# Second feed-forward chunk on two levels of Strassen's scheme, part of the weight conversion on ScalarE and GpSimd, one output block by two adding DMAs

## The chip, the cores and the metric

The kernel runs on one core of a Trainium2 chip. The metric is the device time in microseconds (us) of one execution. Three runs of the kernel before gave 2347.29, 2343.07 and 2347.35 us, a median of 2347.29. The engines named here: TensorE (PE, with its weight loads PEld), VectorE (DVE), ScalarE (ACT), GpSimd (POOL), and SyncE (SP), which only issues DMAs. An engine works off its own instructions in the order in which they were laid down.

## The reference

All data are float32 except two weight matrices, which arrive as float64. For 8 batches of 448 tokens, attention with 12 heads of 64 is computed with a mix over heads before and after the softmax; its result is a tensor x of 8 x 448 x 768. Then:

```
X     = fft(fft(x, axis=1), axis=2)
u     = x + real(X)
un    = (u - mean(u)) / sqrt(var(u) + 1e-6)          # over the last axis
ch    = maximum(un @ w_ch1, 0) @ w_ch2               # w_ch1 768 x 3072, w_ch2 3072 x 768
out   = u + ch
```

The change lies in the last two lines, the feed-forward part.

## The kernel before, in words

`mix_phase` computes the attention, the Fourier mix and u, and writes u to DRAM. It fills the first 812 us of the span, up to the first matmul of line 1169. `ffn_phase` does the rest.

**Tiling.** The 3072 hidden features are cut into NC = 6 chunks (index c), the 3584 tokens into NTB = 7 blocks of 512 (index t). The loop runs over n = 7c + t: chunk by chunk, and inside a chunk block by block. One such n is called a step.

**A step** has two halves. `first` (lines from 1144 on) multiplies a block of normalized tokens, `ub`, with a chunk of w_ch1, `w1`. It uses one level of Strassen's scheme (in Winograd's form): seven products in the order `ORDER`, each of 12 matmul records of 256 columns (line 1169) and accumulated in three kinds of PSUM banks, P, Q and R. Between the products ScalarE copies banks out or applies Relu, and VectorE adds (L1187, L1190, L1195). From the four blocks of h it then forms sums (L1215, L1216, L1219, L1230). The second half multiplies h with a chunk of w_ch2, `w2`:

- `second`, for chunks 0 and 1, does seven products of 384 columns (L1249). In chunk 0 VectorE adds each to the tokens' u (L1256), and SyncE stores the result to the output. In chunk 1 ScalarE and VectorE collect blocks in tiles `od` (L1265 to L1269), and GpSimd sends each by a DMA that adds to what lies in the output (L1271).
- `second2`, for chunks 2 to 5 (`c >= DEEP`, `DEEP = 2`), splits each of the seven products again by Strassen's scheme: 7 x 7 = 49 products of 192 columns (L1306). For this it needs quarters' sums of h (tiles `hq`, function `quarters`, L1133, by VectorE and GpSimd) and, once per chunk, sums of w2 (tiles `wt`, function `halves`, L1142: four subtractions for each of the seven, alternately on VectorE and GpSimd, in the chunk's first step). ScalarE empties most banks into `od` tiles (`take`, L1334; `begin`, L1325), VectorE adds the others (`more`, L1328) and sums whole `od` tiles (`both`, L1337), and GpSimd sends four adding DMAs (`out_`, L1340). `second2` lays its work down in numbered slots, one matmul a slot; slots from 49 on are interleaved with the next step's `first` (`SEAM`, `beside`). `od` has nine buffers.

**The weights' conversion.** The class `_Weights` turns float64 weights into float32 and forms the seven Strassen operands; the result goes to DRAM and is loaded a chunk later by `load_w1` and `load_w2`. A *part* is one 128-row slice of a chunk: three parts for w1 and two for w2 per chunk. A part has four *pieces* of 128 x 256 (w1) or 128 x 384 (w2). Each piece is loaded raw (`load`, L225, `ahead` pieces in advance) and takes seven VectorE operations on its high and low words: absolute value of the high word (`begin`, L247), range limits (`clamp`, L251), shift (L255), sign (L261), power (L265), low word (L269), sum (L273). Four sums per part (L279) follow, and stores to DRAM (L233). These VectorE operations stand in a list; `deal(k)` lays down the next k of them. In chunks 2 to 5, `DEALS` says how many follow each product of `first`, for a chunk's first step and for the others. The parts of chunk 1 are worked in chunk 0, and later parts as lists run short. The raw loads and stores are GpSimd's DMAs up to chunk 1 and SyncE's after that (`wts.eng`).

**What sets the order.** In the two-level steps the order on TensorE, VectorE, ScalarE and GpSimd is the one written in the program; SyncE's DMAs, and before that ScalarE and GpSimd too, are placed by a planner that goes by its own estimates of when something is ready. The first step of the feed-forward part fixes TensorE, VectorE, GpSimd and SyncE; then, up to the end of chunk 1, only TensorE and VectorE are fixed.

Of the kernel before, what the change touches and what calls it, by code (L numbers as in the profile page):

```python
# [165 lines left out]
class _Weights:  # L166
# [14 lines left out]
    def open(self, ctx, tc, ahead=1):  # L181
        self.ahead = ahead
# [4 lines left out]
        self.praw, self.ptmp, self.pst = pool("wraw", ahead + 1), pool("wtmp", 1), pool("wst", 1)  # L187
# [24 lines left out]
    def add(self, c, n):  # L212
# [25 lines left out]

        def begin(k):
# [6 lines left out]
            box["top"] = new(slot)  # L246
            vec.tensor_scalar(box["tmp"].bitcast(U32), box["hi"], 0x7fffffff, None,  # L247
                              op0=ALU.bitwise_and)

        def clamp():  # L250
            vec.tensor_scalar(box["tmp"], box["tmp"], _f32(0x38000000),  # L251
                              _f32(0x47efffff), op0=ALU.max, op1=ALU.min)

        def shift():
            vec.tensor_scalar(box["top"].bitcast(U32), box["tmp"].bitcast(U32),  # L255
                              0x07ffffff, 3, op0=ALU.bitwise_and,
                              op1=ALU.logical_shift_left)
# [23 lines left out]

        self.ops.append((lambda: load(k0 + self.ahead - 1), False))
# [718 lines left out]
DEEP = 2  # L1001
DEALS = ((0, 2, 2, 2, 2, 0, 0), (2, 3, 3, 3, 3, 0, 0))
# [5 lines left out]
def ffn_phase(ctx, tc, rest, ident, u_scr, u_rev, wts, ub_scr, out, fold_rest,  # L1008
# [14 lines left out]
    wts.open(ctx, tc, 3)  # L1023
    once = ExitStack()

# [118 lines left out]
    def first(n, st, beside):  # L1144
# [12 lines left out]
        for k, i in enumerate(ORDER):  # L1157
# [54 lines left out]
            elif i != 2:  # L1212
                wts.deal(2 if norms else 3 if c == 0 else 4)
# [19 lines left out]
    def second(n, st):  # L1233
        c, t = divmod(n, NTB)
        h = st["h"]
        u = us[t] if c == 0 else None
        os = {}
        norms = c == 0 and t + 1 < NTB
# [4 lines left out]
        for k, i in enumerate(ORDER):  # L1243
            for x in range(NT2 // 2):
# [3 lines left out]
                for kf in range(FM):  # L1248
                    nc.tensor.matmul(p, h[:, LHS[i], kf, x * P:(x + 1) * P],  # L1249
                                     w2[i][:, kf, :], start=i in (0, 4, 1)[:3 - (c > 0)] and kf == 0,  # L1250
                                     stop=kf == FM - 1, skip_group_check=True)
                r, d = DEST[i]
                last = i in (1, 6, 2, 3)
                if c == 0:
                    us_ = u[2 * r + x][:, d * DH:(d + 1) * DH]
                    nc.vector.tensor_tensor(us_, us_, p, op=ALU.add)  # L1256
                    if last:
                        nc.sync.dma_start(out=acc[t, r, d][:, x, :], in_=us_)
                    continue
                if (r, d) not in os:  # L1260
                    os[r, d] = right["od"].tile([P, 2, DH], F32, name="od", tag="od")
                o = os[r, d][:, x, :]
                if i == 0:
                    q = ps["Q", x] = ps_tile("Q")
                    nc.scalar.copy(out=q[:, :DH], in_=p)  # L1265
                elif i in (4, 5, 1, 3):
                    nc.scalar.copy(out=o, in_=p)
                else:
                    nc.vector.tensor_tensor(o, o, p, op=ALU.add)  # L1269
                if last and x == 1:  # L1270
                    nc.gpsimd.dma_start(out=acc[t, r, d], in_=os[r, d][:, :, :],  # L1271
                                        accum_op=ALU.add)
# [6 lines left out]
            if n == 0 and k > 2:  # L1279
                next_part()  # L1280
            wts.deal(2 if norms and k >= NT2 else 4)
            if t == NTB - 1:
                load_w2(c + 1, i)

    def second2(n, st):
# [119 lines left out]
    for n in range(DEEP * NTB):  # L1405
        c, t = divmod(n, NTB)
# [13 lines left out]
        if c == 0:  # L1420
            wts.deal(1000)
# [102 lines left out]
```

## Time and profile before

The profile is of one execution of 2343.49 us, of which its span is 2341.7 us.

| what | us |
|---|---|
| median of the runs | 2347.29 |
| profiled execution | 2343.49 |
| its span | 2341.7 |
| PE busy in the span | 2281.3 |
| DVE, ACT, POOL busy | 1677.4, 1101.0, 1140.6 |
| chunk 1, first product's end to the same of chunk 2 | 1111.98 to 1365.94 |
| chunk 2, likewise | 1365.94 to 1609.89 |
| chunk 3, likewise | 1609.89 to 1852.26 |

Busy time by stage, in us, by windows of the trace:

| window | PE | DVE | ACT | POOL | DMA share |
|---|---|---|---|---|---|
| 1109.2 to 1363.2 (chunk 1) | 253.64 | 181.34 | 62.25 | 98.93 | 0.84 |
| 1366 to 1610 (chunk 2) | 241.63 | 173.62 | 104.87 | 88.90 | 0.64 |
| 1610 to 1852 (chunk 3) | 239.34 | 177.13 | 104.65 | 93.02 | 0.64 |
| 1852 to 2094 (chunk 4) | 239.95 | 181.45 | 105.04 | 96.08 | 0.64 |
| 2094 to 2341 (chunk 5) | 237.62 | 142.36 | 103.57 | 98.11 | 0.51 |

How to read the rows that follow: a group's row names line, engine, operation, written tile and read tiles, shapes, the count, busy time and mean. A row of the timeline gives start and length in us, then the same, and in brackets how long the engine was idle before it and what ended that. A float32 matmul appears as two records. A TensorE row that ends a little after the next one starts is normal, since matmuls are pipelined. The profile's line numbers are those of the kernel before.

### The profile page before, as it was taken

How to read it: one execution, taken by the hardware profiler on the slowest of the kernel's cores; microseconds unless marked ns; L12 is line 12 of the kernel's file. 1: busy time of each engine (PE TensorE's matmuls, PEld its weight loads, DVE VectorE, ACT ScalarE, POOL GpSimd, SP SyncE). 2: the span in 40 equal slices, each digit the busy share in tenths (PEclk: the TensorE clock that was granted, in tenths of full speed). 3: DMA queues.
4: the chain of work that ended last, by engine and by line, in shares of the span. 5: the costliest groups of instructions: out<-in, count | busy, mean ns of one | idle time of the engine just before them, and what ended most of it. 6: DMA issues, size and time to landing. Idle time of an engine off the chain costs nothing.

```text
span 2341.7 us, 59482 instructions
## 1 busy us (share of the span) xinstructions
PE 2281.3 (97%) x22600; PEld 1717.1 (73%) x22600; DVE 1677.4 (72%) x3596; ACT 1101.0 (47%) x3085; POOL 1140.6 (49%) x1692
## 2 busy tenths in 40 slices
PE   6999999999999989999999999999999999999998
PEld 3455555555555667676777779998999899999998
DVE  3778887887887747775676766778776777776556
ACT  4776767676676522221222234344344344444434
POOL 3587967878778622210343443335333533443333
PEclk9999999999999999999999999999999999999999
DMA  7565664756656475658787966648645955684553
GB/s 159 157 181 175 182 175 152 205 168 182 186 156 198 146 242 181 220 185 298 209 229 211 270 202 180 161 135 259 172 123 159 267 128 156 176 236 103 147 129 67
DMA packets 213481, 425.60 MB, mean 182 GB/s; under 512 B 39080, under 2 KB 135744, under 8 KB 213198
## 3 DMA queue, kind: packets, MB, share of 16 engines
q1 hardware_dynamic: 141758, 278.78, 35.0%
q0 software_dynamic: 65440, 141.05, 27.5%
q8 instruction: 181, 2.97, 0.5%
q10 hardware_dynamic: 6000, 1.97, 0.5%
q14 instruction: 102, 0.84, 0.1%
HBM read 213.16 MB, written 129.39 MB: 146 GB/s over the span
## 4 chain that ended last, share of the span: by engine, by line
PE 87%; DMA 4%; DVE 4%; ACT 2%; issue 1%; POOL 1%; SPq 1%; ACTq 0%; DVEq 0%; POOLq 0%
PE psP L1169 18%; PE psP L1306 10%; PE psR L1169 9%; PE mx L616 6%; PE psP L1249 6%; PE ms L680 6%; PE ms L588 5%; PE psR L1306 5%; PE psQ L1169 5%; PE po L650 5%; PE psR L1249 3%; DMA Kr<-Sb 3%; PE psQ L1306 3%; PE ms L805 2%; PE psQ L1249 1%; PE ms L562 1%
## 5 line engine op out<-in xcount | busy, mean ns | idle before, releaser
L640 POOL TENSOR_SCALAR PP<-PP,rcp 128x448 f32<-128x448 f32 x368 | 235.2, 648 | 196.8 <-DVE rcp L638 165.6
L630 ACT ACTIVATE PP<-mx,nmx 128x448 f32<-128x448 f32 x368 | 230.2, 631 | 186.5 <-DVE nmx L623 176.2
L623 DVE TENSOR_REDUCE nmx<-mx 128x1 f32<-128x448 f32 x368 | 213.4, 618 | 128.6 <-PE mx L616 126.3
L1340 POOL DMA_DIRECT2D out_dram<-od x109 | 133.1, 1406 | 283.5 <-DVE od L1337 160.2
L1133 POOL TENSOR_TENSOR hq<-h 128x256 f32<-128x256 f32 (+1 forms) x168 | 104.6, 623 | 291.0 <-ACT h L1191 171.5
L1337 DVE TENSOR_TENSOR od<-od 128x768 f32<-128x768 f32 x196 | 189.0, 975 | 52.4 <-ACT od L1334 50.5
L616 PE MATMUL mx<-Kr,kw 60*32 60x448 f32 x2944 | 212.5, 549 | 11.6 <-DMA Kr<-Sb 11.1
L588 PE MATMUL ms<-kT,qT 64*32 64x448 f32 (+1 forms) x3072 | 202.7, 547 | 8.6 <-ACT qT L451 6.0
L663 DVE STREAM_TRANSPOSE Pv<-po 128x896 f32<-128x896 f32 x184 | 203.8, 1108 | 4.3 <-PE po L650 2.1
L451 ACT COPY Sb<-ms 124x448 f32<-124x448 f32 (+1 forms) x384 | 184.3, 540 | 36.4 <-PE ms L588 23.7
L650 PE MATMUL po<-PP,kw 60*32 60x448 f32 x2944 | 195.7, 538 | 0.0
L1334 ACT COPY od<-psP 128x192 f32<-128x192 f32 x390 | 124.8, 320 | 147.2 <-PE psP L1306 142.9
L680 PEld LDWEIGHTS ms<-Pv,vv 64*64 64x64 f32 x5376 | 137.1, 132 | 68.9 <-issue 52.3
L225 POOL DMA_DIRECT2D raw<-in_moe_w_ch_dram x88 | 52.1, 592 | 264.6 <-DVE tmp L269 247.2
L1169 PE MATMUL psP<-qs,w1t 128*128 128x256 f32 x744 | 177.3, 379 | 0.0
L1169 PE MATMUL psP<-ks,w1t 128*128 128x256 f32 x744 | 176.8, 379 | 0.1
L680 PE MATMUL ms<-Pv,vv 64*64 64x120 f32 (+1 forms) x5376 | 158.9, 263 | 0.0
L1249 PE MATMUL psP<-w2t,h 128*128 128x384 f32 x448 | 155.5, 491 | 0.4 <-DVE od L1269 0.4
L1169 PEld LDWEIGHTS psP<-ks,w1t 128*128 128x128 f32 x744 | 139.9, 190 | 18.5 <-DVE u L1256 0.7
L1169 PEld LDWEIGHTS psP<-qs,w1t 128*128 128x128 f32 x744 | 139.8, 190 | 17.5 <-issue 0.2
L1190 DVE TENSOR_TENSOR h<-h,psP 128x512 f32<-128x512 f32 x42 | 28.8, 687 | 142.0 <-PE psP L1169 141.8
L1169 PE MATMUL psP<-ub,w1t 128*128 128x256 f32 x528 | 126.4, 379 | 0.0
(194 smaller groups left out, 5127.4 us busy)
## 6 DMA issues: line engine op xcount, KB each, us to landing
Kr<-Sb SPq DMA_DIRECT2D x736, 105.0 KB
out_dram<-od POOLq DMA_DIRECT2D x137, 384.0 KB, 6.3
qs<-ub SPq DMA_DIRECT2D x89, 384.0 KB
ks<-ub SPq DMA_DIRECT2D x88, 384.0 KB
ub<-ub SPq DMA_DIRECT2D x79, 384.0 KB
w1t<-w SPq DMA_DIRECT2D x42, 384.0 KB
w2t<-w SPq DMA_DIRECT2D x42, 384.0 KB
raw<-in_moe_w_ch_dram POOLq DMA_DIRECT2D x56, 256.0 KB, 4.4
```

The source lines that it names most:

```text
L588: nc.tensor.matmul(pss[x][o:o + hi - lo, :S], st["qT", xx][64 * x:64 * x + 64, y, lo:hi], st["kT", xx][64 * x:64 * x + 64, y, :], start=Tr ...
L616: nc.tensor.matmul(mx[x][64 * z + o:64 * z + o + 32, :S], kw1[64 * x:64 * x + KR, o:o + 32], Kr[64 * x:64 * x + KR, z, :], start=True, sto ...
L623: nc.vector.tensor_reduce(nmx[:, :], steps[T]["mx"][x][:, :S], axis=AX.X, op=ALU.max, negate=True)
L630: nc.scalar.activation(steps[T]["PP"][:, x, :], steps[T]["mx"][x][:, :S], ACTF.Exp, bias=steps[T]["nmx", x][:, :], accum_out=steps[T]["den ...
L640: nc.gpsimd.tensor_scalar(PP[:, x, :], PP[:, x, :], rcp[:, x:x + 1], 1.0, op0=ALU.mult, op1=ALU.mult)
L650: nc.tensor.matmul(po[o:o + 32, z, :S], kw2[64 * z:64 * z + KR, y, :], PP[64 * z:64 * z + KR, :, c * HS:(c + 1) * HS], start=True, stop=True)
L663: nc.vector.transpose(turned[a]["Pv"][:, j, :].rearrange("p (z s) -> p z s", z=2), steps[T]["po"][:, :, :S])
L680: nc.tensor.matmul(pss[y][64 * x:64 * x + 64, :nu * R], st["v", pr][64 * y:64 * y + 64, x, jb * D:(jb + 1) * D], _ap(Pv, 64 * y * rp + 32 ...
L1169: mm = nc.tensor.matmul(p[:, m, :], w1[i][:, kc, m * P:(m + 1) * P], ub[:, kc, :], start=i in (0, 4, 1)[:3 - seed] and m == kc == 0, stop= ...
L1249: nc.tensor.matmul(p, h[:, LHS[i], kf, x * P:(x + 1) * P], w2[i][:, kf, :], start=i in (0, 4, 1)[:3 - (c > 0)] and kf == 0, stop=kf == FM ...
L1306: nc.tensor.matmul(ps[j, key][:, :DQ], a, b, start=m in (0, 4), stop=True, skip_group_check=True)
L1337: eng.tensor_tensor(D[j][:, :, :], D[j][:, :, :], D[k][:, :, :], op=ALU.add)
```

## The change

Four things are changed together.

1. `DEEP` goes from 2 to 1, so chunk 1 too uses `second2`; `second` then serves chunk 0 alone, and its branch for chunk 1 is deleted. The tiles for two levels were opened ahead of chunk 1 before, and still are.
2. `_Weights` gets a mode `split`, used from chunk 1 on. A piece's absolute value is made by ScalarE (`Abs`, straight into the piece's tile), its range limits are set by GpSimd in place, and the other five operations stay on VectorE. The two new operations of a piece are laid down when the piece two before it begins on VectorE. The weight pools are closed and opened again behind chunk 0, with five raw buffers for four, raw loads four pieces ahead instead of three, and two buffers for each finished tile instead of one.
3. The deals change: `DEALS` rises to 10 operations in a chunk's first step and 18 in the others (8 and 14 before), chunk 0 takes one part in each step from 1 to 6 (1 to 5 before), and parts are added when the list is shorter than 36 instead of 14.
4. Output block 21 (`(1, 0)` in the code) is the sum of `j3` and `j6`. Before, VectorE added the two and one DMA added the sum to the output. Now `j3` and `j6` are each sent by an adding DMA, at slots 27 and 44, and block 22 is summed in `j4` instead of `j6`. The last step of all is as before.

```diff
+    def open(self, ctx, tc, ahead=1, split=False):
+        self.ahead, self.split = ahead, split
...
+        self.pst = pool("wst", 1 + split)
...
+        def early(k):
+            _, f, slot = ps[k]
+            top = new(slot)
+            tops.append(top)
+            nc.scalar.activation(top, self.raws[k0 + k][:, :f, 1].bitcast(F32), ACTF.Abs)
+            clamp(nc.gpsimd, top)
+
         def begin(k):
             _, f, slot = ps[k]
             load(k0 + k + self.ahead)
...
+            if self.split:
+                while self.pre and self.pre[0][0] <= k0 + k + 2:
+                    self.pre.pop(0)[1]()
+                box["top"] = tops[k]
+            else:
+                box["top"] = new(slot)
+                size(vec, box["hi"], box["tmp"])
...
-            self.ops.append((lambda k=k: begin(k), True))
-            for fn in (clamp, shift, sign, power, lower, whole):
+            self.ops.append((lambda k=k: begin(k), not self.split))
+            if not self.split:
+                self.ops.append((lambda: clamp(vec, box["tmp"]), True))
+            self.ops.append((lambda: shift(vec, box["top" if self.split else "tmp"],
+                                           box["top"]), True))
+            for fn in (sign, power, lower, whole):
...
-DEEP = 2
-DEALS = ((0, 2, 2, 2, 2, 0, 0), (2, 3, 3, 3, 3, 0, 0))
+DEEP = 1
+DEALS = ((2, 2, 2, 2, 2, 0, 0), (3, 4, 4, 4, 3, 0, 0))
...
-    wts.open(ctx, tc, 3)
     once = ExitStack()
+    wts.open(once, tc, 3)
...
             for s, *o in ((33, j5, j0), (40, j6, j5), (47, j5, j4), (54, j0, j1),
-                          (61, j5, j2), (62, j3, j6), (63, j6, j4)):
+                          (61, j5, j2), (62, j4, j6)):
                 on(s, both, vec, *o)
+            on(27, out_, j3, 1, 0)
+            on(44, out_, j6, 1, 0)
             on(55, out_, j0, 0, 0)
             on(62, out_, j5, 0, 1)
-            on(63, out_, j3, 1, 0)
-            on(64, out_, j6, 1, 1)
+            on(63, out_, j4, 1, 1)
...
-    for n in range(DEEP * NTB):
-        c, t = divmod(n, NTB)
-        if c == 0 and 0 < t < NK + FM + 1:
-            wts.add(*parts_.pop(0))
-        while c and sum(o[1] for o in wts.ops) < 52:
+    for n in range(NTB):
+        if n:
             wts.add(*parts_.pop(0))
...
         if n == NTB - 1:
             once.close()
+            wts.open(ctx, tc, 4, True)
...
-            while parts_ and sum(o[1] for o in wts.ops) < 14:
+            while parts_ and sum(o[1] for o in wts.ops) < 36:
```

More of the change, by code (lines that the diff above doesn't have):

```diff
@@ L179, in __init__ @@
         self.ops, self.pieces, self.raws, self.later = [], [], {}, []
-    def open(self, ctx, tc, ahead=1):
-        self.ahead = ahead
+        self.pre = []
+    def open(self, ctx, tc, ahead=1, split=False):
+        self.ahead, self.split = ahead, split
         def pool(name, bufs):
@@ L186, in pool @@
                                                   reuse_waits="tile"))
-        self.praw, self.ptmp, self.pst = pool("wraw", ahead + 1), pool("wtmp", 1), pool("wst", 1)
+        self.praw, self.ptmp = pool("wraw", ahead + 1), pool("wtmp", 1)
+        self.pst = pool("wst", 1 + split)
     def _parts(self, c):
@@ L233, in store, with size, clamp, shift @@
             self.later.append(lambda: self.eng.dma_start(out=dst[slot], in_=box[slot]))
+        def size(eng, hi, tmp):
+            eng.tensor_scalar(tmp.bitcast(U32), hi, 0x7fffffff, None,
+                              op0=ALU.bitwise_and)
+        def clamp(eng, tmp):
+            eng.tensor_scalar(tmp, tmp, _f32(0x38000000), _f32(0x47efffff),
+                              op0=ALU.max, op1=ALU.min)
+        def shift(eng, tmp, top):
+            eng.tensor_scalar(top.bitcast(U32), tmp.bitcast(U32), 0x07ffffff, 3,
+                              op0=ALU.bitwise_and, op1=ALU.logical_shift_left)
+        def early(k):
[4 more added lines that the diff above has]
+            clamp(nc.gpsimd, top)
         def begin(k):
@@ L245, in begin @@
             box["slot"] = slot
[L246 to L257, printed above, removed]
+            if self.split:
[5 more added lines that the diff above has]
+                size(vec, box["hi"], box["tmp"])
         def sign():
@@ L280, in total @@
             store(o)
+        tops = []
+        if self.split:
+            self.pre.extend((k0 + k, lambda k=k: early(k)) for k in range(len(ps)))
         self.ops.append((lambda: load(k0 + self.ahead - 1), False))
         for k in range(len(ps)):
-            self.ops.append((lambda k=k: begin(k), True))
-            for fn in (clamp, shift, sign, power, lower, whole):
+            self.ops.append((lambda k=k: begin(k), not self.split))
[4 more added lines that the diff above has]
+            for fn in (sign, power, lower, whole):
                 self.ops.append((fn, True))
@@ L1212, in first @@
             elif i != 2:
-                wts.deal(2 if norms else 3 if c == 0 else 4)
+                wts.deal(2 if norms else 3)
             if i == 2:
@@ L1231, in first, with second @@
         assert not beside
-    def second(n, st):
-        c, t = divmod(n, NTB)
[L1235 to L1238, printed above, removed]
+    def second(t, st):
+        h, u = st["h"], us[t]
+        norms = t + 1 < NTB
         if norms:
@@ L1249, in second @@
                     nc.tensor.matmul(p, h[:, LHS[i], kf, x * P:(x + 1) * P],
-                                     w2[i][:, kf, :], start=i in (0, 4, 1)[:3 - (c > 0)] and kf == 0,
+                                     w2[i][:, kf, :], start=i in (0, 4, 1) and kf == 0,
                                      stop=kf == FM - 1, skip_group_check=True)
                 r, d = DEST[i]
[L1253 to L1272, printed above, removed]
+                us_ = u[2 * r + x][:, d * DH:(d + 1) * DH]
+                nc.vector.tensor_tensor(us_, us_, p, op=ALU.add)
+                if i in (1, 6, 2, 3):
+                    nc.sync.dma_start(out=acc[t, r, d][:, x, :], in_=us_)
             if norms and k < NT2:
@@ L1278, in second @@
                 total(t + 1, k - NT2 + 1)
-            if n == 0 and k > 2:
+            if t == 0 and k > 2:
                 next_part()
@@ L1282, in second @@
             if t == NTB - 1:
-                load_w2(c + 1, i)
+                load_w2(1, i)
     def second2(n, st):
@@ L1404, in ffn_phase @@
     parts_ = [(c, k) for c in range(1, NC) for k in range(NK + FM)]
-    for n in range(DEEP * NTB):
-        c, t = divmod(n, NTB)
-        if c == 0 and 0 < t < NK + FM + 1:
-            wts.add(*parts_.pop(0))
-        while c and sum(o[1] for o in wts.ops) < 52:
+    for n in range(NTB):
+        if n:
             wts.add(*parts_.pop(0))
@@ L1419, in ffn_phase @@
         second(n, st)
-        if c == 0:
-            wts.deal(1000)
+        wts.deal(1000)
         if n == 0:
```

## The prediction

> **What bounds the kernel now.** I began with the page's shares and its list of costliest groups. TensorE is busy for 97% of the span, so a change pays only if it shortens TensorE's work or removes or adds a stall of TensorE.
>
> ```profile
> PE 2281.3 (97%) x22600; PEld 1717.1 (73%) x22600; DVE 1677.4 (72%) x3596; ACT 1101.0 (47%) x3085; POOL 1140.6 (49%) x1692
> ```
>
> Next came the chain that ended last, for the pace of one token step. A row here is start, length, and twelve matmul records, that is one product of the first matrix; the same tile recurs once a step.
>
> ```profile
> 1254.15 2.59 PE psP L1169 x12
> ...
> 1290.34 2.59 PE psP L1169 x12
> ...
> 1438.67 2.59 PE psR L1169 x12
> ...
> 1472.88 2.59 PE psR L1169 x12
> ```
>
> In feed-forward chunk 1 a step takes 1290.34 - 1254.15 = 36.19 us; in chunk 2, which already runs two levels, 1472.88 - 1438.67 = 34.21 us (34.20 over most pairs). This agrees with the timeline: one product of the first matrix is 2.59 us, so seven are 18.13; seven one-level second products of 2.58 us are 18.06; the 49 small ones start 0.325 us apart, 15.93 in all. The two-level form is thus shorter on this array by about 2.0 us a step, though it issues 49 matmuls of 192 columns for 28 of 384.
>
> Last came TensorE's own waits in the two-level chunks, by its timeline. The bracket holds the idle time and what ended it.
>
> ```profile
> 1387.90 0.59 PE L1306 MATMUL psP<-wt,h 128*128 128x192 f32 x2 [2.37 <-DVE od L1328]
> 1632.14 0.59 PE L1306 MATMUL psP<-wt,h 128*128 128x192 f32 x2 [2.66 <-DVE od L1328]
> 1873.89 0.59 PE L1306 MATMUL psP<-wt,h 128*128 128x192 f32 x2 [2.05 <-DVE od L1328]
> 2115.41 0.59 PE L1306 MATMUL psP<-wt,h 128*128 128x192 f32 x2 [1.82 <-DVE od L1328]
> ```
>
> There is one such stall per two-level chunk, always in its first step, where VectorE works off four extra subtractions (L1142) behind the sums of h before it can empty a PSUM bank. Chunk 5 has no weight pieces left to convert and still stalls 1.82 us; the others lose 2.05 to 2.66. No other step of these chunks waits, but for the last at the very end.
>
> **Part 1, chunk 1 on two levels.** Seven steps at 36.19 - 34.20 = 1.99 us: 13.9 us gained. Against it stands the first step. From psR to psR the steps that hold a stall last 38.53 (n = 14), 37.14, 36.52 and 36.29 us, that is 4.3, 2.9, 2.3 and 2.1 over 34.20. At n = 14 the excess is more than its 2.37 us of idle: the matmuls behind the gap are 0.64 us apart instead of 0.325, for 3 us.
>
> ```profile
> 1389.83 0.85 PE L1306 MATMUL psR<-w2t,hq 128*128 128x192 f32 x2
> 1390.47 0.85 PE L1306 MATMUL psP<-w2t,h 128*128 128x192 f32 x2
> ```
>
> The granted clock of 1380 to 1400 us is 0.91 as a mean, while the stall of 2.66 us cost only itself. The Trainium skill ("TensorE: Matmul & The Clock Gate", section "Why this matters for your kernels") asks only that idle gaps stay under about 3 us; by it the new first step would cost 2.4 and the part would bring 11.5 before the seams. The row shows that 2.4 us of idle can bring half rate, so I go by the row. I price the first step of chunk 1 like n = 14 (4.3), which loads a fresh set of weights behind a one-level chunk just the same; n = 14 becomes an ordinary one (2.9), and the 0.63 us that chunk 1 lost at its own end goes (1111.98 to 1365.94 is 253.96; seven steps are 253.33). Sum: 13.9 - 4.3 + (4.3 - 2.9) + 0.6 = **11.6 us gained**. The same from chunk lengths: 253.96 + 243.95 before, 243.95 + 242.37 after.
>
> **Part 2, weight pieces off VectorE.** Of 25 parts, 6 are now done in chunk 0; 19 parts of 4 pieces, 76 pieces, are left. Each sheds two VectorE operations, 0.29 + 0.29 us uncontended at 256 columns (0.36 + 0.36 at 384), and gains one ScalarE and one GpSimd operation. Abs has no row. The nearest is the 128x384 copy, 478 ns (L1267); [...]0.5 to 1 us, and I take 0.5. A table load before each Abs would be the bad bound: the one load in the trace took 1.28 us, and two per piece would be 195 us. I count none: one load serves Exp, Copy, Relu and Identity here, and the skill ("ScalarE: Activation LUTs", "Table sets: the hidden batching unit") lists abs in every set. The clamp on GpSimd I take from L640, 648 ns for 448 columns: 0.4 to 0.6 us. Some 2.2 pieces a step mean 1.1 us more on ScalarE (43% busy, 104.65 of 242 us in chunk 3) and 1.2 on GpSimd (38%).
>
> What does this do on TensorE's path? VectorE must be ready for h22 when product 6 ends. Its spare time there is shown by its timeline, with eleven weight operations dealt before it and with none:
>
> ```profile
> 1725.93 0.69 DVE L1190 TENSOR_TENSOR h<-h,psP 128x512 f32<-128x512 f32 x1 [4.36 <-PE psP L1169]
> ...
> 2140.79 0.69 DVE L1190 TENSOR_TENSOR h<-h,psP 128x512 f32<-128x512 f32 x1 [7.72 <-PE psP L1169]
> ```
>
> The new deal is fifteen there, from the dearer kinds: 15 x 0.37 = 5.5 us (256 columns) or 15 x 0.48 = 7.2 (384). With one 0.96 us sum less (part 3), 7.72 + 0.96 - 5.5 = 3.2 or 1.5 us is spare. VectorE is slowed while GpSimd works (L1142 on VectorE takes 0.74 us beside GpSimd, 0.35 alone), but 1.2 us of clamps cannot eat more than the rest. So ordinary steps: zero. In first steps ten operations replace eight, one sum goes: +4.0 - 2.9 - 0.96 = +0.1 us per chunk, between -0.5 and +1; I take zero. If the cover went, every late microsecond would delay h21's sums and so the bank that product 0 waits for, as in the rows above.
>
> The waits that come with it: an Abs stands on ScalarE behind its raw load, and the PSUM copies stand behind the Abs. Its load is issued four pieces ahead and the Abs runs two ahead, so in one step the load has ten VectorE operations' room, some 5 to 8 us; raw loads landed in 4.4 us (median). The Abs that can be short of data fall in products 5 and 1, when ScalarE's next item is a Relu with over 2 us to spare. Zero, with the bad end in the rivals.
>
> **Part 3, block 21.** One 128x768 sum on VectorE goes (0.96 us a step, off the path), an accumulating DMA of 384 KB is added to each two-level step but the last. Its issue costs GpSimd 1.22 us, at slots 27 and 44, where GpSimd is idle:
>
> ```profile
> 1714.28 1.21 POOL L1340 DMA_DIRECT2D out_dram<-od  x1 [9.38 <-DVE od L1337]
> ```
>
> Both DMAs add to the same bytes. The skill ("DMA: Bandwidth & Descriptors", "Two DMAs through the same engine are not ordered") says that a queue does not order them and the issuer has to wait for the first to land; that speaks against the edit. The row: landing takes 6.3 us, the issues are 17 x 0.325 = 5.5 us apart, so GpSimd, with the sum block for j0 behind it at slot 55, would stand about 2 us of some 9 idle. By rule and by row the sum gets zero; uncovered it would be 2 us a step. The DMA engines are 64% busy in chunks 2 to 4 and 84% in chunk 1, whose four adding DMAs become five: no stage is DMA-bound.
>
> **Part 4, the seam from chunk 0.** Chunk 0 takes one more part in its last step, about 32 x 0.45 = 14 us of VectorE where it now has an 8 us gap and GpSimd 37.75 us; zero. Afterwards the pools are reopened, so the chain of raw load, Abs, clamp, shift starts empty in step 7. The SP queue issues the last w2 load of chunk 0 at 1109.42, TensorE begins step 7 at 1109.39; if the raw loads follow and land like the w2 load of the other seam,
>
> ```profile
> 1347.27 9.19 DMA w2t<-w
> ```
>
> the first piece is there at about 1118.6. ScalarE's Abs would hold h21's copy, due 1119.6, by about a microsecond; VectorE would start its ten dealt operations (3.7 us), two sets of L1142 (3 to 4) and two sums (1.4) then, ending near 1127.5 against 1124.9, when h21's product ends: 2.6 us late. If the planner puts the raw loads ahead of the waiting w2 loads, as it did at 1363.85, it is nothing. Also, the planner may pull the first L1142 set into chunk 0's tail (in the trace VectorE stood 5.36 us for w2 at the other seam, which cost TensorE 0.36). Bounds 0 and 8; I take **1.5 us lost**.
>
> **Sum.** 11.6 - 1.5 = 10.1 us. In the profiled execution 2343.5 (span 2341.7 and 1.8 around it) becomes 2333.4; against the median of 2347.3, which lies 3.8 above that execution, **2337.2**.
>
> **Rivals.** (a) The seam is dear: step 7 stalls 8 us for raw and w2 data and a further half-rate stretch follows, while the first steps of all chunks grow by 1 us: 11.6 - 8 - 2 gives 2346, at best 2342. For it: 2.7 MB of w2 and 1 MB of raw in one place; against: chunk 1's own start shows no wait. (b) ScalarE becomes the gate, and the kernel is slower. Place: products 0 to 4 of each step, Abs waiting for raw data on SP behind ub loads that keep TensorE's pace (one per 2.59 us). If the Abs delays PSUM copies so that TensorE loses 0.33 us in each of 35 steps, the gain is gone; at 0.8 us it is 28 - 11.6, near 2364. For it: load and Abs are only two pieces apart; against: ScalarE's idle of about 2 us between copies in every product. (c) More is gained: the first-step stall falls to chunk 5's 1.82 everywhere and no half rate follows; 11.6 + 3.4 gives 2332. (d) Part 1 saves nothing since the array is not the limit: the step times of 36.19 and 34.20 speak against it; folded into (a).
>
> **How the numbers follow.** Forecast 0.63 (its own range 2333 to 2342), (c) 0.06, (a) with (d) 0.18, of which 0.12 still faster, 0.05 the same, 0.01 slower; (b) 0.13, of which 0.02 the same, 0.11 slower. About 0.2%, 4.7 us, is what a measurement can tell from no change. Faster 0.81, same 0.07, slower 0.12. The range must take in the forecast and nearly all of (a): 2332.5 to 2346; it leaves out (b) and some of (c).
>
> **What would show it.** Chunk 1's steps at 34.20; one stall before a `psP<-wt,h` matmul in step 7 and in each later first step, 1.8 to 2.7 us; VectorE idle before L1190's counterpart at 1.5 to 3.2 us; no table load but the first; GpSimd waiting for a landing at slot 44 with nobody behind. Wrong if TensorE waits for ScalarE copies in ordinary steps, or if step 7 loses over 8 us.

## The result, and the profile after

The kernel after takes 2334.98 us (median of 17 runs, 2326.71 to 2340.21); the kernel before, run on the same chips beside it, takes 2344.55 us (17 runs). The ratio is 0.9954 with a 95% interval of 0.9942 to 0.9967: faster by 0.46%. Applied to the 2347.29 us of the runs shown before, that is 2336.5 us; predicted were 2337.2. The profiled execution of after lasts 2333.72 us, with a span of 2332.0, that is 9.7 less than before. Line numbers below are those of the kernel after, in which L1310 is the matmul of the second level (L1306 before), L1192 the product of the first matrix (L1169), L1332 `more` (L1328) and L1213 the sum of h22 (L1190).

The shares of the page:

```profile
PE 2272.2 (97%) x22894; PEld 1752.2 (75%) x22894; DVE 1704.3 (73%) x3629; ACT 1176.3 (50%) x3336; POOL 1279.8 (55%) x1783
```

TensorE has 294 matmul records more (two for each of 147 matmuls) and is busy 9.1 us less. GpSimd, busy for 139 us more, is the engine that took the work. The chain that ended last shows the pace of chunk 1 (start, length, twelve records of one product):

```profile
1289.77 2.59 PE psR L1192 x12
...
1323.97 2.59 PE psR L1192 x12
```

These are the same product in two successive steps: 34.20 us, where the kernel before took 36.19 there. TensorE's stalls, from its timeline (the bracket is the idle time before the row and what ended it), are again one per first step of a chunk, now five (what it waits for in the very last step is left out):

```profile
1136.39 0.78 PE L1310 MATMUL psP<-wt,h 128*128 128x192 f32 x2 [2.27 <-DVE od L1332]
1379.62 0.59 PE L1310 MATMUL psP<-wt,h 128*128 128x192 f32 x2 [1.81 <-DVE od L1332]
1621.22 0.92 PE L1310 MATMUL psP<-wt,h 128*128 128x192 f32 x2 [1.91 <-DVE od L1332]
1864.41 0.59 PE L1310 MATMUL psP<-wt,h 128*128 128x192 f32 x2 [1.81 <-DVE od L1332]
2105.91 0.59 PE L1310 MATMUL psP<-wt,h 128*128 128x192 f32 x2 [1.80 <-DVE od L1332]
```

They are about as short as chunk 5's was before (1.82), except the one at n = 7. Two of the five are followed by matmuls at half rate. Busy time by windows around the first three of these rows (length, then busy time of PE, PEld, DVE, ACT and POOL, granted clock, DMA share, GB/s) shows which:

```profile
1130.00:1142.00 12.00, 9.73 (x48) 9.22 (x47) 10.49 (x24) 5.46 (x18) 9.47 (x17) 0.86 0.14 50
1375.00:1387.00 12.00, 10.19 (x62) 9.71 (x61) 10.21 (x28) 6.71 (x22) 6.65 (x12) 1.00 0.24 67
1617.00:1629.00 12.00, 10.09 (x51) 9.79 (x51) 9.04 (x24) 5.62 (x18) 7.13 (x12) 0.86 0.25 71
```

In 12 us TensorE has some 50 matmul records at a mean granted clock of 0.86 and 62 at 1.00.

**A yardstick.** The part ahead of step 7 is the same program but for one weight part, and it is not the same length twice: the first matmul of h's second product in step 7 (tile psQ) came at 1115.7 to 1122.4 us in all traces but one. A span therefore compares to some 3 us only. I use the time from that matmul of step 7 to that of step 41, 34 steps. At 34.205 us each, which is what a two-level step without a stall takes, they would be 1163.0 us; what is above that is loss.

| kernel | ratio to before (95%) | span, us | 34 steps, us |
|---|---|---|---|
| before | 1 | 2341.7 | 1189.34 |
| after | 0.9954 (0.9942 to 0.9967) | 2332.0 | 1177.30 |
| part 1 alone | 1.0231 (1.0205 to 1.0258) | 2387.3 | 1235.15 |
| part 1 alone, two buffers | 1.0045 (1.0029 to 1.0060) | 2349.8 | 1193.80 |
| block 21 summed on VectorE | 0.9949 (0.9932 to 0.9966) | 2337.9 | 1177.75 |
| clamp done twice | 0.9963 (0.9943 to 0.9984) | 2337.8 | 1180.14 |
| clamp replaced by two multiplications | one run | 2335.3 | 1178.04 |
| clamp with one limit | one run | 2328.1 | 1173.70 |
| late sums of w2, in a lump | 0.9937 (0.9917 to 0.9957) | 2331.5 | 1173.78 |
| late sums of w2, spread | 0.9921 (0.9903 to 0.9938) | 2315.8 | 1164.67 |
| late sums of w2, spread, GpSimd's too | 0.9914 (0.9896 to 0.9933) | 2317.8 | 1163.62 |

Between before and after the 34 steps lose 12.04 us. The span lost 9.7, since the front of the after trace happened to be 2.5 us longer.

### The profile page after: what moved, and what is told of

It reads as the page before. It is cut to its first block, busy times and chain, and to the rows that moved or that the text cites. A ratio compares the mean times of both kernels' runs of the same rounds, so it can differ in the third digit from the quotient of the medians.

```text
span 2332.0 us, 60769 instructions
## 1 busy us (share of the span) xinstructions
PE 2272.2 (97%) x22894; PEld 1752.2 (75%) x22894; DVE 1704.3 (73%) x3629; ACT 1176.3 (50%) x3336; POOL 1279.8 (55%) x1783
## 4 chain that ended last, share of the span: by engine, by line
PE 88%; DMA 4%; DVE 3%; ACT 2%; SPq 1%; issue 1%; POOL 0%; ACTq 0%; DVEq 0%; POOLq 0%
PE psP L1192 18%; PE psP L1310 13%; PE psR L1192 9%; PE mx L639 7%; PE psR L1310 7%; PE ms L703 6%; PE ms L611 6%; PE po L673 5%; PE psQ L1192 5%; PE psQ L1310 3%; PE psP L1269 3%; DMA Kr<-Sb 3%; PE ms L828 2%; PE ms L585 1%; PE psR L1269 1%; PE ms L812 1%
## 5 line engine op out<-in xcount | busy, mean ns | idle before, releaser
L1344 POOL DMA_DIRECT2D out_dram<-od x171 | 207.8, 1275 | 261.3 <-DVE od L1332 167.9
L1156 POOL TENSOR_TENSOR hq<-h 128x128 f32<-128x128 f32 (+1 forms) x210 | 128.1, 610 | 262.9 <-ACT h L1214 127.6
L1338 ACT COPY od<-psP 128x192 f32<-128x192 f32 x488 | 156.4, 321 | 182.0 <-PE psP L1310 177.5
L1341 DVE TENSOR_TENSOR od<-od 128x768 f32<-128x768 f32 x211 | 201.7, 969 | 53.9 <-ACT od L1338 52.9
L639 PE MATMUL mx<-Kr,kw 60*32 60x448 f32 x2944 | 217.4, 551 | 9.1 <-DMA Kr<-Sb 8.5
L1192 PE MATMUL psP<-ks,w1t 128*128 128x256 f32 x744 | 179.1, 379 | 0.1
L1192 PE MATMUL psP<-qs,w1t 128*128 128x256 f32 x744 | 179.0, 379 | 0.0
L246 POOL TENSOR_SCALAR wst<-wst 128x256 f32<-128x256 f32 (+1 forms) x76 | 119.0, 1574 | 67.7 <-ACT wst L257 66.4
L1192 PEld LDWEIGHTS psP<-ks,w1t 128*128 128x128 f32 x744 | 139.4, 190 | 16.7 <-DVE u L1274 0.7
L1192 PEld LDWEIGHTS psP<-qs,w1t 128*128 128x128 f32 x744 | 139.5, 190 | 16.5 <-issue 0.2
L1310 PE MATMUL psP<-wt,h 128*128 128x192 f32 x490 | 120.8, 328 | 11.7 <-DVE od L1332 11.7
L1192 PE MATMUL psP<-ub,w1t 128*128 128x256 f32 x528 | 127.0, 379 | 0.0
L1213 DVE TENSOR_TENSOR h<-h,psP 128x512 f32<-128x512 f32 x42 | 28.8, 687 | 130.2 <-PE psP L1192 112.7
```

Of the source, the lines that this page charges most:

```text
L639: nc.tensor.matmul(mx[x][64 * z + o:64 * z + o + 32, :S], kw1[64 * x:64 * x + KR, o:o + 32], Kr[64 * x:64 * x + KR, z, :], start=True, sto ...
L1192: mm = nc.tensor.matmul(p[:, m, :], w1[i][:, kc, m * P:(m + 1) * P], ub[:, kc, :], start=i in (0, 4, 1)[:3 - seed] and m == kc == 0, stop= ...
L1310: nc.tensor.matmul(ps[j, key][:, :DQ], a, b, start=m in (0, 4), stop=True, skip_group_check=True)
L1341: eng.tensor_tensor(D[j][:, :, :], D[j][:, :, :], D[k][:, :, :], op=ALU.add)
L1344: nc.gpsimd.dma_start(out=acc[t, r, d], in_=D[j][:, :, :], accum_op=ALU.add)
```

## The experiments

**Part 1 alone.** Chunk 1 on two levels, everything else as before: all seven weight operations on VectorE, one buffer for each finished tile, block 21 summed on VectorE. The deals are raised so that the conversion keeps its schedule.

```diff
-DEALS = ((2, 2, 2, 2, 2, 0, 0), (3, 4, 4, 4, 3, 0, 0))
+DEALS = ((2, 3, 3, 3, 3, 0, 0), (4, 6, 6, 6, 4, 0, 0))
...
-            wts.open(ctx, tc, 4, True)
+            wts.open(ctx, tc, 4)
...
-            while parts_ and sum(o[1] for o in wts.ops) < 36:
+            while parts_ and sum(o[1] for o in wts.ops) < 58:
...
-                          (61, j5, j2), (62, j4, j6)):
+                          (61, j5, j2), (62, j3, j6), (63, j6, j4)):
...
```

> Chunk 1 on two levels, but the weights' conversion all on VectorE again (seven operations a piece) and block 21 summed by VectorE with one adding DMA. The deals must then be 14 in a first step and 26 in the others, 22 of them ahead of the sum for h22. Theory A (TensorE's own work sets the time; parts 2 and 3 only keep VectorE off the path): 22 operations take 22 x 0.36 = 7.9 us at 256 columns and 22 x 0.48 = 10.6 us at 384, against 7.7 us of spare time, so VectorE is up to 3 us late in the steps that convert 384-column pieces (8 of 19 parts) and TensorE loses 0 to 2 us there: 5 to 20 us in all, first-step stalls 2.5 to 3.5 us. Ratio to the kernel before 0.998 to 1.004: parts 2 and 3 are what lets part 1 pay. Theory B (parts 2 and 3 are ornament, VectorE has room): ratio 0.995 to 0.996 as with the whole change.

The 34 steps take 1235.15 us, 45.8 more than before and 57.9 more than after: worse than either theory expected. Its waits (engine, tile and line that waited, what for, total, times, longest), of TensorE and then of VectorE:

```profile
PE psP L1310 <- DVE od L1332: 19.2, 16, 2.8
PE psP L1310 <- ACT psQ L1329: 17.0, 8, 4.8
...
PE psP L1192 <- DVE h L1213: 15.8, 4, 5.8
```

```profile
DVE wst L250 <- DMA w<-wst: 39.4, 7, 6.9
```

TensorE now waits in ordinary steps as well, and for the sums of h themselves (L1213). Behind it VectorE stood seven times, up to 6.9 us, until a finished weight tile had gone to DRAM and its only buffer was free. So this run does not measure the number of operations alone; the next one separates the two.

**Part 1 with two buffers.** The same with a second buffer for each finished tile.

```diff
-        self.pst = pool("wst", 1 + split)
+        self.pst = pool("wst", 2 if ahead > 3 else 1)
```

> As the run with part 1 alone (seven operations a piece on VectorE, block 21 summed by VectorE), but with two buffers for each finished weight tile, as the change has them. In the first run VectorE stood 6 to 7 us at a shift for the store of the part before (single buffers), which leaves open whether the operations or the buffers cost the time. Theory A (the buffers did it): the long waits of VectorE for stores go, and TensorE loses at most 15 us; ratio to the kernel before 0.995 to 1.002. Theory C (the number of operations on VectorE did it): ratio stays above 1.010, with waits of TensorE for h22's sum and for banks in ordinary steps.

1193.80 us: of the 57.9 us, 41.4 were the single buffer, and 16.5 remain for the operations on VectorE, block 21's sum among them (the wait for the store is gone from VectorE's list). Each theory named one cause, and the ratio of 1.0045 lies between their ranges: both causes are there. TensorE's waits:

```profile
PE psP L1310 <- DVE od L1332: 14.5, 13, 2.8
PE psP L1310 <- ACT psQ L1329: 5.2, 6, 1.1
```

Thirteen waits for `more`, where after has one per first step, and six for a copy that ScalarE makes late. One of these six, followed back: first VectorE's rows of that step, then TensorE's.

```profile
1232.93 0.68 DVE L1213 TENSOR_TENSOR h<-h,psP 128x512 f32<-128x512 f32 x1
...
1236.43 0.67 DVE L1218 TENSOR_TENSOR h<-h,psR 128x512 f32<-128x512 f32 x1
```

```profile
1238.13 0.56 PE L1310 MATMUL psP<-wt,hq 128*128 128x192 f32 x2 [0.95 <-ACT psQ L1329]
```

The sum of h22 has no bracket: VectorE came to it straight from weight pieces, 1.65 us after its product had ended (1231.28). The next sum (L1218), behind four more weight operations, starts 2.6 us after its own product (1233.87). ScalarE's Relu waits for that sum, its copy stands behind the Relu, and the copy holds TensorE for 0.95 us. Chunk 1 by windows, after and then this run:

```profile
1114.50:1358.20 243.70, 241.43 (x1276) 224.65 (x1275) 187.09 (x403) 113.58 (x316) 126.54 (x151) 0.99 0.77 207
```

```profile
1114.50:1358.20 243.70, 238.71 (x1264) 220.51 (x1263) 204.09 (x453) 104.32 (x292) 87.52 (x120) 1.00 0.67 195
```

VectorE is busy 204 us of 244 instead of 187. As an average that is still only 84%; in the rows above, what costs the time is that the operations stand in front of the sums of h. With all operations on VectorE, dealt like this, chunk 1 on two levels is thus no gain but a loss: 4.5 us in the 34 steps against before, and 0.45% of the time. Other deals were not tried, nor was the move of operations without chunk 1 on two levels.

**Block 21 summed on VectorE.** From after, only block 21 is put back.

```diff
-                          (61, j5, j2), (62, j4, j6)):
+                          (61, j5, j2), (62, j3, j6), (63, j6, j4)):
...
-            on(27, out_, j3, 1, 0)
-            on(44, out_, j6, 1, 0)
...
-            on(63, out_, j4, 1, 1)
+            on(63, out_, j3, 1, 0)
+            on(64, out_, j6, 1, 1)
```

> The changed kernel with part 3 undone: block 21 is summed on VectorE (0.96 us a step more) and sent by one adding DMA. Theory A (part 3 is worth nothing on TensorE's path): within 1.5 us of the changed kernel, ratio to the kernel before 0.995 to 0.996; first-step stalls 1.8 to 2.6 us, ordinary steps 34.20. Theory B (VectorE is at its limit in the first half of a step, and the sum's 0.96 us is seen): 0.3 to 0.96 us in each of 35 steps, 10 to 33 us, ratio 0.999 to 1.010.

0.45 us in 34 steps, and the ratios' intervals lie on each other: the third part is worth nothing that can be measured. The 0.45 is a difference of two effects, though. With the sum back on VectorE the first steps n = 7, 14 and 28 are 0.8, 0.8 and 0.5 us longer and one other step 0.2, while n = 21 is 1.9 shorter, since no half rate follows its stall in this trace. So in first steps the sum may cost some 2 us; one trace of each kernel does not settle it.

This run showed something else, at the end of chunk 0. TensorE's row and VectorE's row from its timeline:

```profile
1108.82 2.85 PE L1269 MATMUL psP<-w2t,h 128*128 128x384 f32 x8 [1.28 <-DVE ur L1274]
```

```profile
1107.74 0.36 DVE L1165 TENSOR_TENSOR wt<-w2t 128x192 f32<-128x192 f32 x1 [3.77 <-DMA w2t<-w]
```

VectorE stood 3.77 us in chunk 0's last step, waiting for chunk 1's w2 to form its sums (L1165), and the add that frees a PSUM bank (L1274) stood behind. The step is 37.74 us long instead of 36.19. In after the same step is 36.19.

**Clamp done twice.** After gives GpSimd 76 clamps (L246). Here each is done a second time, with the same output.

```diff
             clamp(nc.gpsimd, top)
+            clamp(nc.gpsimd, top)
```

> The changed kernel with GpSimd's range limits applied twice to each piece (the second time without effect), 1.6 us more GpSimd work per piece, 3.5 us per step. Theory A (GpSimd's work on the pieces is covered by some 9 us that it is idle in a step): under 3 us in all, ratio 0.995 to 0.997. Theory C (the clamps are close to being the gate, since VectorE already waits for them six times ahead of h22's sum, 16 us in all): VectorE is late for h22 by 1 to 3 us in most steps, 15 to 60 us, ratio 1.00 to 1.02.

1180.14 us, 2.84 more than after. Step 7 is 3.4 us longer (41.85 against 38.43), where the chain of raw load, Abs, clamp and shift starts empty, and half rate lasts 6.83 us there instead of 3.41; n = 14 is 0.75 us longer and three ordinary steps 0.2 to 0.3 each; n = 21, where no half rate follows this time, is 2.2 shorter. TensorE's stall in step 7 has a new releaser, a sum of h's quarters that GpSimd makes:

```profile
1137.49 1.01 PE L1311 MATMUL psR<-wt,hq 128*128 128x192 f32 x2 [2.41 <-POOL hq L1157]
```

The group of clamps grows from 119.0 to 216.1 us. These 97 us of GpSimd work cost 2.8 us, and 5.1 without the luck at n = 21; 0.9 of that falls in ordinary steps. There the cover that the prediction named for this part is real, and large. The expectation's theory C reads six waits of VectorE ahead of h22's sum as waits for a clamp. In after's timeline these six sums start 0.13 or 0.14 us after their product has ended, as the others do, so it was the product that ended the wait.

**Other work in the clamp's place.** The clamp turned out to be slow (below), so I measured what its operation costs, by two forms that compute something else: two multiplications by 1.0, which leave both range limits out, and a maximum alone, which leaves the upper limit out.

```diff
-            clamp(nc.gpsimd, top)
+            nc.gpsimd.tensor_scalar(top, top, 1.0, 1.0, op0=ALU.mult, op1=ALU.mult)
```

> The changed kernel, but GpSimd multiplies each piece by one twice in place of the two range limits (the limits are left out; the operation keeps its shapes and its place). In the changed kernel this operation took 1.57 us as a mean, 1.06 at the least for 256 columns, where the forecast had 0.4 to 0.6 from a multiply of 448 columns in 0.65. Theory A (maximum and minimum are dear on GpSimd, multiply is not): mean falls to 0.4 to 0.8 us. Theory B (the place makes it slow: VectorE beside it, or the buffers): stays above 1.2 us. The time of the whole kernel stays within 3 us of the changed kernel in both.

```diff
-            clamp(nc.gpsimd, top)
+            nc.gpsimd.tensor_scalar(top, top, _f32(0x38000000), None, op0=ALU.max)
```

> The changed kernel with the lower limit alone on GpSimd (the upper limit is left out). Theory A (each of maximum and minimum is dear): mean about half of 1.57 us, 0.7 to 0.9. Theory B (the place makes it slow): stays above 1.2 us.

The groups by form (count, busy time, mean ns; then idle time before and what ended it), of after, of the multiplications and of the one limit:

```profile
L246 POOL TENSOR_SCALAR wst<-wst 128x256 f32<-128x256 f32 x44 | 63.2, 1442 | 35.9 <-ACT wst L257 34.7 <-DMA w<-wst 1.1
L246 POOL TENSOR_SCALAR wst<-wst 128x384 f32<-128x384 f32 x32 | 55.8, 1756 | 31.9 <-ACT wst L257 31.8
```

```profile
L258 POOL TENSOR_SCALAR wst<-wst 128x256 f32<-128x256 f32 x44 | 32.9, 748 | 44.8 <-ACT wst L257 44.4 <-DMA raw<-in_moe_w_ch_dram 0.3
```

```profile
L258 POOL TENSOR_SCALAR wst<-wst 128x256 f32<-128x256 f32 x44 | 53.4, 1214 | 38.8 <-ACT wst L257 38.7
```

A piece of 256 columns takes 1442 ns with two limits, 1214 with one, 748 with two multiplications: the limits are dear. The 1214 are well above the 0.7 to 0.9 us of the last expectation's theory A and just above the mark of its theory B, since the place has its share too. The four or five pieces of each group beside which VectorE was idle for most of the time took 1.07, 0.85 and 0.40 us in the mean, the others 1.48, 1.26 and 0.78: VectorE beside it adds some 0.4 us to each of the three operations, and the limits cost what is left. Yet 63 us less GpSimd work in the second run of the three changed the 34 steps by +0.74 us, so GpSimd's time is free here in this direction as well. The one-limit run took 3.6 us less than after, but hardly through GpSimd: steps n = 7 and n = 21 account for all of it, since no half-rate stretch fell into the 34 steps of this trace. At n = 7 its gap is even longer than after's, and the granted clock of the 12 us around it (the window's row, columns as above) is full:

```profile
1136.16 0.59 PE L1310 MATMUL psP<-wt,h 128*128 128x192 f32 x2 [2.39 <-DVE od L1332]
```

```profile
1130.00:1142.00 12.00, 9.61 (x59) 9.13 (x58) 11.20 (x27) 6.67 (x22) 9.47 (x16) 1.00 0.11 34
```

**Late sums of w2, in a lump.** What remains in after is the first step's stall. The prediction puts it down to the extra subtractions on w2 that VectorE does behind h's sums and ahead of the first bank. This set, the last of the seven (`ORDER2[6]`), belongs to the products from slot 42 of the second half on, so it need not stand there. Here it moves to slot 24.

```diff
-            if deep and t == 0:
+            if deep and t == 0 and k < 6:
...
+        if t == 0:
+            on(24, halves, ORDER2[6], vec)
```

> The changed kernel, but in a chunk's first step the last set of four subtractions of w2 on VectorE is laid down at slot 24 of the second half instead of ahead of it; its result is needed at slot 42. Theory A (these four subtractions, 1.8 to 2.6 us, are the stall of every first step, and the half-rate stretches follow from that idle time): the five waits of 1.81 to 2.27 us go or fall under 0.5 us, and with them the stretches at half rate behind two of them; 9.6 us and 3 to 4 us less, span near 2319, ratio to the kernel before 0.989 to 0.992. Theory B (the bank waits for the sums of h and for GpSimd's interference, and the subtractions only happen to lie there; or the stall moves to slot 24): less than 3 us gained, ratio above 0.994.

At the old place the stall is gone; it reappears at the new one, where four subtractions in one lump stand ahead of `more`:

```profile
1386.15 0.59 PE L1310 MATMUL psP<-wt,h 128*128 128x192 f32 x2 [1.18 <-DVE od L1332]
```

1173.78 us, with stalls of 2.25, 1.18, 1.46, 1.17 and 1.18 us: 3.5 less than after, of which 2.1 come from n = 21 (35.94 us for 38.06), where the stall of 1.46 is followed by no half rate. Theory A had the cause, but its 13 us did not come; the clause of theory B that the stall moves to slot 24 did. The subtractions are thus what holds the bank up, and in one lump they do so from their new place too.

**Late sums, spread, and GpSimd's too.** First the same set cut into single subtractions at slots 25, 25, 30 and 32; then also the set of `ORDER2[5]`, GpSimd's, at slot 20.

```diff
-            if deep and t == 0:
+            if deep and t == 0 and k < 5:
...
+        if t == 0:
+            on(20, halves, ORDER2[5], pl)
+            for x, s in enumerate((25, 25, 30, 32)):
+                on(s, halves, ORDER2[6], vec, x, x + 1)
```

The first of the two has `k < 6` and no line for slot 20; in both, `halves` takes the range of subtractions that it is to do.

> The changed kernel with the last set of four subtractions of w2 on VectorE moved behind the first products' banks and spread over slots 25, 25, 30 and 32, where the lump at slot 24 had made a new stall of 1.2 us. Theory A (the four subtractions are the stall; in small pieces they fit in VectorE's gaps): no wait over 0.6 us in any first step but the first of chunk 1, no half-rate stretch in the two-level chunks; 3 to 6 us less than the lump, span near 2326, ratio 0.989 to 0.993. Theory B (VectorE has no spare time at all in the first half of a first step, so the stall only moves on): waits of 1 us and more remain at later slots, ratio 0.993 to 0.996.

> As the run before, and GpSimd's last set of four subtractions is moved to slot 20 too, so that GpSimd no longer works beside VectorE's sums of h, which take 0.56 us beside it against 0.28 alone. Theory A (what is left of the wait is the mutual slowing of VectorE and GpSimd): all waits in first steps under 0.3 us, 0.5 to 1 us less per chunk than the run before, ratio 0.988 to 0.992. Theory B (no effect, or GpSimd is then late with block sums): same as the run before within 1.5 us.

1164.67 and 1163.62 us against the 1163.0 of a kernel without a stall. The first steps last 35.14, 34.45, 34.21, 34.44 and 34.42 us in the first run, 34.82 and four times 34.21 in the second (the 0.6 us left at n = 7 are in no wait that the profile lists). The second run's list of all that TensorE waits for from 1115 us to the end has only the last step's waits:

```profile
PE psP L1311 <- DVE od L1333: 2.5, 2, 2.1
```

In both runs no half-rate stretch is left from step 7 to the last step, and the gain over the lump, 9.1 us in the 34 steps for the first of the two, is more than the 3 to 6 expected. The step from the first to the second fits theory A by its waits and theory B by its size: 1.05 us in all, since little was left to gain. What GpSimd's move changed is seen in VectorE's sums of h's quarters at n = 14, the first of four in the one run and in the other:

```profile
1367.47 0.57 DVE L1156 TENSOR_TENSOR hq<-h 128x128 f32<-128x128 f32 x1
```

```profile
1370.08 0.29 DVE L1156 TENSOR_TENSOR hq<-h 128x128 f32<-128x128 f32 x1
```

The second run is the best version measured: 2320.52 us beside 2340.09 for the kernel before on the same chip, 0.9914 (0.9896 to 0.9933). It beats both kernels; over the first of the two its lead is within the intervals.

## Why the prediction was right, step by step

**Part 1 (predicted 11.6 us gained): right in mechanism and size, the size in part by luck.** By the same steps, as measured in the traces:

| term | predicted | measured |
|---|---|---|
| seven steps 1.99 us shorter | +13.9 | +13.9 (34.20 a step) |
| stall of the new first step, n = 7 | -4.3 | -4.2 |
| n = 14 becomes an ordinary first step | +1.4 | +2.2 (38.53 to 36.29) |
| loss at chunk 1's end goes | +0.6 | +0.6 |
| n = 21 | 0 | -0.9 (37.14 to 38.06) |
| n = 28, 35 and one other step | 0 | +0.5 |
| sum | 11.6 | 12.1 |

Two terms were off in opposite directions, by 0.8 and 0.9 us; that they cancel is luck. Relieving VectorE did what rival (c) supposed: the stalls fell to chunk 5's floor of 1.8 us in three of five first steps. But at n = 21 a gap that is shorter than before (1.91 for 2.66 us) now brings half rate. The matmuls behind it start 0.64 us apart instead of 0.325:

```profile
1621.93 0.85 PE L1310 MATMUL psR<-wt,hq 128*128 128x192 f32 x2
1622.57 0.85 PE L1310 MATMUL psP<-wt,hq 128*128 128x192 f32 x2
```

The prediction went by the row at n = 14 rather than by the rule of the Trainium skill ("TensorE: Matmul & The Clock Gate", section "Why this matters for your kernels"), that gaps under about 3 us leave the clock alone. At n = 7 and n = 21 the runs are with the row: 2.27 and 1.91 us sufficed, and the step was 4.2 and 3.9 us longer. By the rule the two stalls would have cost 2.3 and 1.9. (The table takes each step as it is, so n = 7 has all that happened there; see part 4.)

**Part 2 (predicted zero on ordinary steps): right, and for the reason given, with one term badly sized.** Abs takes 439 and 555 ns, as taken (0.5 us). ScalarE loads its tables once (one load of 1.28 us in the whole trace). VectorE's spare time ahead of h22, by its timeline:

```profile
1231.83 0.69 DVE L1213 TENSOR_TENSOR h<-h,psP 128x512 f32<-128x512 f32 x1 [1.73 <-PE psP L1192]
...
1575.99 0.69 DVE L1213 TENSOR_TENSOR h<-h,psP 128x512 f32<-128x512 f32 x1 [3.83 <-PE psP L1192]
...
2131.29 0.69 DVE L1213 TENSOR_TENSOR h<-h,psP 128x512 f32<-128x512 f32 x1 [8.71 <-PE psP L1192]
```

It is 1.6 to 3.8 us in the ordinary steps with fifteen operations dealt (predicted 1.5 to 3.2) but for 0.69 in one, and 8.71 with none, which is the 7.72 of before and the 0.96 of the sum that went. TensorE waits for ScalarE in none of them; that would have been the sign that the prediction was wrong. The clamp is the mis-sized term: 0.4 to 0.6 us from L640, measured 1.44 and 1.76: L640 multiplies, and the run with two multiplications in the clamp's place came to 0.75. The sum did not feel it, since, as the doubled clamp shows, GpSimd's time there is covered. What the prediction did not price is how much this "zero" carries: without parts 2 and 3, and with the second buffer kept, the 34 steps take 16.5 us more and the kernel is slower than before. In that sense the gain hangs on part 2, though its own line in the sum is nought.

**Rival (b), ScalarE as the gate, has fallen.** Over the window in which pieces are worked, Abs waited for raw data 3.8 us in all at one size (all of it in step 7) and not at all at the other:

```profile
L257 ACT ACTIVATE wst<-raw 128x256 f32<-128x256 f32 x44 | 19.3, 439 | 3.9 <-DMA raw<-in_moe_w_ch_dram 3.8
L257 ACT ACTIVATE wst<-raw 128x384 f32<-128x384 f32 x32 | 17.8, 555 | 0.0
```

**Part 3 (predicted zero): right.** GpSimd did stand at slot 44 with the second adding DMA. In three steps the profile names the first DMA's landing as what ended the wait. One of them, GpSimd's two issues and VectorE's sum into `j6` between them:

```profile
1313.58 1.22 POOL L1344 DMA_DIRECT2D out_dram<-od  x1
1319.61 1.20 POOL L1344 DMA_DIRECT2D out_dram<-od  x1 [4.81 <-DMA out_dram<-od]
```

```profile
1316.90 0.96 DVE L1341 TENSOR_TENSOR od<-od 128x768 f32<-128x768 f32 x1 [0.32 <-ACT od L1338]
```

Of the 4.81 us, 3.1 pass until `j6` has its sum (1317.86); the other 1.7 are the landing, where 2 were predicted. As predicted, nobody stood behind it who was needed. The adding DMAs landed in 4.9 to 12.2 us, 6.8 as a median.

**Part 4, the seam (predicted 1.5 lost): the term that failed.** Step 6 is 36.19 us, and TensorE waits for no load in step 7. The first raw piece was not queued behind w2 as in the row I took (9.2 us); SyncE issued it in front (start, length):

```profile
1111.60 0.42 SPq L227 DMA_DIRECT2D raw<-in_moe_w_ch_dram  x1
1113.18 0.42 SPq L1098 DMA_DIRECT2D w2t<-w  x1
```

```profile
1116.64 0.43 ACT L257 ACTIVATE wst<-raw 128x256 f32<-128x256 f32 x1 [1.49 <-DMA raw<-in_moe_w_ch_dram]
```

Abs had its data 5.0 us after the issue. This was the milder case that the prediction named and did not take. VectorE still stood for the first piece, but came to h22's sum only 0.74 us after its product had ended (1124.89), not 2.6 us late, and was on time again for the next sum:

```profile
1118.29 0.29 DVE L250 TENSOR_SCALAR wst<-wst 128x256 uint32<-128x256 uint32 x1 [5.76 <-POOL wst L246]
...
1125.63 0.67 DVE L1213 TENSOR_TENSOR h<-h,psP 128x512 f32<-128x512 f32 x1
```

What the seam leaves in step 7 comes by another way, which the prediction did not have. GpSimd waited 9.3 us for the first Abs, and its last set of w2 sums ended 11.0 us after h22's product instead of 7.7 (n = 14). So it ran beside VectorE's last four subtractions, which took 2.7 us instead of 1.9, and the stall of n = 7 is 2.27 us where the other four are 1.80 to 1.91. These 0.4 us, and their part in whether half rate followed, lie within part 1's term for n = 7; no run separates them.

The other path that the prediction named, an Abs that holds h21's copy on ScalarE, is in the trace as well:

```profile
1119.18 0.44 ACT L257 ACTIVATE wst<-raw 128x256 f32<-128x256 f32 x1 [2.12 <-DMA raw<-in_moe_w_ch_dram]
...
1120.67 0.60 ACT L1206 COPY h<-psP 128x512 f32<-128x512 f32 x1
```

The copy comes 1.1 us after the 1119.6 at which it was due, as predicted. But it ends at 1121.3, and TensorE's next product into a bank of this kind starts at 1122.1. In two other runs that slack was too short: in step 7 TensorE waits for this copy 0.40 us with the clamp done twice and 0.27 us with the late sums in a lump. The other half of the term, sums of w2 pulled into chunk 0's tail, is real as well: the run with block 21 on VectorE shows it at 1.55 us. That run changed nothing at the seam, so it was most likely the planner's choice; no run tests that.

**In sum**, the steps brought 12.0 us, with what the seam cost in n = 7 already taken off, where a gain of 11.6 and a loss of 1.5 were predicted. The median moved by 9.6 and the profiled execution by 9.8. That the predicted 10.1 comes so close is in part luck: the steps brought 1.9 more than the predicted sum, and the part ahead of step 7 was 2.5 longer in after's trace. Whether the change or the spread of executions made it longer, nothing here tells: the matmul that the yardstick starts from came at 1117.0 us in the one trace of before and at 1115.7 to 1124.4 in the ten others.

## What to carry to other kernels

Price a move of work between engines by what stands in front of the critical operation, not by the share of busy time: 17 us more of VectorE work in chunk 1, enough of it ahead of h22's sum, turned a gain into a loss, while 97 us more on GpSimd behind a slack cost 3 to 5. Before an experiment takes one part of a change alone, look at what buffers came with the other parts; here the missing second buffer cost more (41.4 us) than the effect in question (16.5). And when every step of a kind runs at the array's pace, look for work in the exceptional step that can be done later: four subtractions, moved behind the first banks and spread, brought 12.6 us in the 34 steps, as much again as the whole change. In one lump they brought 3.5.

## What the runs showed of the hardware

**Half rate comes in fixed windows.** In every trace the stretches at half rate last 3.413 us or a multiple of it (but the last, which the end of the trace cuts off), and their starts fit a grid of 3.413 us: in after at 1136.66 and 1621.35 us, 142 windows apart (484.69 / 142 = 3.413). I placed TensorE's idle time on this grid in all traces, from 1000 us on. Of the windows at full rate, the fourteen with 2.04 us of idle time or more and one with 1.91 were followed by half rate; those with 1.87 and less were not, and one with 1.95 was not. So a gap of 2.66 us that straddles two windows (1.63 + 1.03, n = 21 of before) costs little more than itself, and one of 1.91 inside a single window costs 1.9 us more. The longer gap of the one-limit run (2.39 us, full clock) agrees: on the grid of that trace, placed by its half-rate stretches elsewhere, it splits into 1.12 + 1.28. So does n = 7 of the lump run (2.25 us, 0.97 + 1.28, no half rate). The rule is read out of the traces; no run moved a gap on purpose to test it, so it is argued, not shown. What is shown is that gaps of about 2 us sometimes halve the rate, and that with the gaps gone (the spread sums) no such stretch was left in the two-level steps before the last.

**Limits on GpSimd are slow.** For 128x256 one maximum costs it 0.84 us at the least and 1.21 in the mean, both limits 1.06 and 1.44, two multiplications 0.39 and 0.75.

**VectorE and GpSimd slow each other.** The first of the 128x128 sums of h's quarters at n = 14 takes VectorE 0.57 us beside GpSimd and 0.29 once GpSimd's set of w2 sums has moved away (the rows above). That move took the last 1.05 us (1164.67 to 1163.62), though no matmul had waited for those GpSimd sums. In the other direction, GpSimd's clamp of 256 columns takes 1.07 us in the mean while VectorE is mostly idle and 1.48 otherwise.
